# One attention and FFN block in float32r: how the mean and scale of two row blocks are turned and stored, and how attention's pieces are dealt to the FFN pairs

## The chip, the cores and the metric

The kernel runs on one core of a Trainium2 chip. The metric is the device time of one execution in microseconds (us). TensorE does the matrix products, VectorE and ScalarE the work by elements, GpSimd a few small operations and part of the DMA issues, SyncE ("SP") most of the DMA issues. In the profile they are PE (with PEld for its weight loads), DVE, ACT, POOL and SP.

## The reference

The block takes x of 2048 rows and 576 columns, normalizes each row, and adds to x an attention and a feed-forward network (FFN) that both read the normalized rows:

```
xn = (x - mean(x)) / sqrt(var(x) + 1e-5)                # per row, 576 columns
q, k, v = split(xn @ wqkv)                              # 32 heads of 18 columns
logits[s, w] = q[s] . k[s - 2 w] * 18**-0.5             # w = 0..7, earlier rows only
A = (softmax over w of logits, times v[s - 2 w]) @ wo
B = relu(xn @ w1 + b1)**2 @ w2 + b2                     # 4608 hidden columns
out = x + A + B
```

All inputs and the output are float32.

## The kernel before

**Blocks and phases.** The 2048 rows are four blocks of 512 (`TB`). The 4608 hidden columns are 36 tiles of 128, taken as 18 pairs (`NP`). The program runs in this order: `open_rows` and `q0` (normalization and QKV of blocks 0 and 1), `phase_a(0)` (18 FFN pairs for blocks 0 and 1 together, with the output products of block 0), `phase_b0` (output products of block 1, then QKV of blocks 2 and 3 in "quads"), `phase_a(1)` (18 FFN pairs for blocks 2 and 3), `phase_b1` and `tail`.

**Products.** Each float32 operand is split into a high and a low float32r part; ScalarE makes the high part and VectorE the low part by subtraction (`w2_hi` and `w2_lo`, `w1_hi` and `w1_lo`, `square_hi` and `square_lo`). A pair's first products for the two blocks are done with seven products instead of eight (slots T1, T2, T3, T4, B11, B21, B22). The 64 columns of xn that are left over after 512 go into a stacked product of their own; its weights are made by `left_w(r)` for four pairs at a time.

**A pair, `ffn_pair(s, p, work)`.** TensorE goes through `product(ba, B11)`, `product(bc, T1)`, `product(bb, T2)`, `product(bb, T3)`, `product(ba, B21)`, then `third()` with `product(bc, B22)` and `fourth()` with `product(bb, T4)`. Between them `work(i)` adds seven output products at a time (line 549). ScalarE's copy of the first product (line 723) comes once in each pair. VectorE combines the next pair's weights (`combine_w1`), makes the low halves (`splits`), and adds `r1[:, 1] = bc + u` after T3; only then can TensorE go on to write the bank `bc` in `third()` (line 653, which waits for `r`).

**Work beside the pairs.** Each engine works through its own queue in program order. Three kinds of work are laid between a pair's steps:
- Attention. One (block, group) pair of eight heads is a generator of 19 steps, each one VectorE instruction of about 128x1152 elements or a few smaller ones (`attention`, lines 380 to 422). `side(k)` runs k steps. In `phase_a(0)` a pair runs `PIECES[p]` steps in its first part, before `splits`, then two in `third()` and two at its end. In the quads a step is run after the numbers listed at line 1241. `complete(b)` runs what is still left of a block. GpSimd issues attention's loads (lines 362 and 364) and its eight stores of `o` (line 420).
- Mean and scale of blocks 2 and 3, `statistics(b)` (lines 169 to 189). `ROWS` (line 45) places its four steps, one row group of 128 rows each: for block 2 in pairs 7, 8 and 9, for block 3 in pairs 11, 12 and 13; the last step lies in `part(0)` of pair 9 or 13. A step is two `bn_stats`, one `bn_aggr`, a copy of the mean, and `inverse_std`: VectorE adds epsilon (line 153), GpSimd raises to the power -0.5 (line 154). After the last step GpSimd issues the store of the whole `mr` (line 184) to `mrscr[b]` in DRAM, which is laid out [8, 128], while `mr` is [128, 8]: the access pattern is turned, so each contiguous piece is one value of 4 bytes. `load_mb(b)` (line 212) reads `mrscr[b]` back, spread to all partitions, before block b is normalized in `phase_b0`.
- The leftover weights. In part 1 of pairs 1, 5, 9 and 13 SyncE issues the load of `in_w1l` (line 602); in part 0 of pairs 2, 6, 10 and 14 VectorE combines them (`left_w`, four instructions), ScalarE makes the high half in part 1, VectorE the low half in part 2, and GpSimd stores both (line 611).

Parts 0, 1 and 2 are the calls `part(i)` within `ffn_pair`; `part(0)` stands before the `PIECES[p]` steps.

Of the kernel before, what the change touches and what calls it, by code (L numbers as in the profile page):

```python
# [8 lines left out]
F32 = mybir.dt.float32  # L9
# [7 lines left out]
P = 128  # L17
# [4 lines left out]
NJ = TB // P  # L22
# [10 lines left out]
L = P // G  # L33
# [9 lines left out]
NS = 7  # L43
PLAIN = 3
ROWS = {(4 * b - 1 + k // 3, k % 3): (b, h) for b in (2, 3) for k, h in ((0, 0), (2, 2), (3, 1), (5, 2), (6, 2))}
PIECES = (0, 0, 1, 2, 2, 3, 1, 3, 2, 2, 1, 2, 1, 0, 2, 2, 4, 4)
STACK = {T1: 0, B11: 1, B22: 2, B21: 3, T3: 4, T2: 5, T4: 6}


# [1 line left out]
def block_kernel(ctx: ExitStack, tc: tile.TileContext, x, xt, wqkv, wo, w1, b1, w2, b2, w1l, out):  # L51
    nc = tc.nc
    const = ctx.enter_context(tc.tile_pool(name="const", bufs=1))
    mt = ctx.enter_context(tc.tile_pool(name="mt", bufs=1))
    sb = ctx.enter_context(tc.tile_pool(name="sb", bufs=1))
# [24 lines left out]
    half = const.tile([P, 1], F32, name="half")  # L80
# [19 lines left out]
    mrscr = {b: dram.tile([2 * NJ, P], F32, name=f"mr{b}") for b in range(2, NB)}  # L100
# [41 lines left out]
    def bn_stats(b, rows, j, k):  # L142
        if k == 0:
            ln[b, j] = sb.tile([P, 2, 6], F32, name="st6", bufs=NJ)
        nc.vector.bn_stats(out=ln[b, j][:, k], in_=rows[:, j, k * 288:(k + 1) * 288])

    def mean_var(b, j):
        mv = sb.tile([P, 2], F32, name="mv", bufs=NJ)
        nc.vector.bn_aggr(out=mv, in_=ln[b, j])
        ln[b, j] = mv  # L150

    def inverse_std(rs, var):
        nc.vector.tensor_scalar(out=rs, in0=var, scalar1=EPS, scalar2=None, op0=ALU.add)
        nc.gpsimd.tensor_tensor(out=rs, in0=rs, in1=half, op=ALU.pow)
# [14 lines left out]
    def statistics(b):  # L169
        mr = sb.tile([P, 2, NJ], F32, name="mr")  # L170
        for j in range(NJ):
            for k in range(2):
                if b == 1:
                    bn_stats(b, rows_of[b], j, k)
                else:
                    if k == 0:
                        ln[b, j] = sb.tile([P, 2, 6], F32, name="st6", bufs=NJ)
                    nc.vector.bn_stats(out=ln[b, j][:, k], in_=rows_of[b][j][:, 0, k * 288:(k + 1) * 288])
            mean_var(b, j)
            nc.vector.tensor_copy(mr[:, 0, j:j + 1], ln[b, j][:, 0:1])  # L180
            inverse_std(mr[:, 1, j:j + 1], ln[b, j][:, 1:2])
            if j == NJ - 1:
                if b > 1:
                    nc.gpsimd.dma_start(mrscr[b].rearrange("n p -> p n"), mr.rearrange("p k j -> p (k j)"))
                mrs[b] = mr
                measured.add(b)
                if b == 1:
                    release()
            yield
# [177 lines left out]
    def release():  # L367
        free[0] += 1
        fetch()

    def offer(b, g=None):
        if g is None:
            loads.append(("x", b, None))
            queue.append((("x", b), lambda: statistics(b)))
        else:
            loads.extend([("k", b, g), ("v", b, g)])
            queue.append((("k", b, g), lambda: attention(b, g)))
        fetch()
# [47 lines left out]
    def side(k, exp=True):  # L426

        while k > 0:
            if current[0] is None:
                if not queue or queue[0][0] not in landed:  # L430
                    return k
                name, make = queue.pop(0)
                current[:] = [make(), None, name]
            if current[1] == "exp" and not exp:
                return k
            try:
                current[1] = next(current[0])
                k -= 1
            except StopIteration:
                current[0] = None  # L440
        return 0
# [188 lines left out]
    def ffn_pair(s, p, work, first=False):  # L630
# [30 lines left out]
        def part(i):  # L661

            if not s and (p, i) in ROWS:
                b, h = ROWS[p, i]
                if h:
                    next(rv["m", b])
                else:
                    rv["m", b] = statistics(b)
                if h < 2:
                    load_two_rows(b, h)  # L670
# [59 lines left out]
        if not first:  # L730
            side(2 + (p > 2) if s else PIECES[p], False)
        work(0)
# [392 lines left out]
    def phase_b0():  # L1125
        b = 1
# [110 lines left out]
        def quads(k, half, some):  # L1237
            for n in some:
                s, i = steps[n]
                quad_step(k, s, 2 * half + i, i)  # L1240
                if n in ((1, 2, 3, 4, 6, 8, 10, 11, 12), (0, 2, 6, 8, 10, 12, 13), (2, 3, 5, 6, 7, 8, 9, 10, 11, 12, 13), (0,))[2 * k + half]:
                    side(1)
                hook(k, half, s, i)

        for k, half in ((0, 0), (0, 1), (1, 0)):
            quads(k, half, range(len(steps)))
        quads(1, 1, range(len(steps) - 2))

        def chunks(*cs):
# [5 lines left out]
        def filler(i):  # L1255
            if i == 0:
                quads(1, 1, [len(steps) - 2])
# [455 lines left out]
    nc.sync.dma_start(b2t, b2)  # L1713
    load_xt(1)
    of_rows = statistics(1)
    open_rows()
    for g in range(G):
# [66 lines left out]
```

## Time and profile before

| | us |
|---|---|
| median of 3 runs | 1126.09 (1122.3 to 1127.82) |
| profiled execution | 1128.06 |
| its span, first to last instruction | 1126.2 |
| TensorE busy | 1099.2 |
| VectorE busy | 888.3 |
| ScalarE busy | 566.9 |
| GpSimd busy | 153.2 |

Mean granted TensorE clock: 0.988. DMA moved 297.32 MB, 264 GB/s in the mean.

In the tables of the trace a row of the timeline gives the start in us from the span's start, the duration in us, the engine, the line of the kernel, the operation, the tiles written and read, and in brackets the idle time of the engine ahead of the instruction and what ended it. A row of the waits gives who waited for whom: us in total, how many times, the longest. A row of DMA issues gives the tiles, the queue, the count, the size of one and the median time from issue to landing. A row of a stretch gives its limits, its length, the busy us of each engine with the number of instructions in brackets, the granted clock, the mean busy share of the 16 DMA engines, and GB/s. A group by line gives busy us in total, mean ns of one, and idle us ahead of it. Busy time of TensorE is modelled, since matmuls are pipelined.

### The profile page before, as it was taken

What the parts mean: (1) busy time and instruction counts of PE and PEld (TensorE: products, weight loads), DVE (VectorE), ACT (ScalarE), POOL (GpSimd) and SP (SyncE); (2) the same over time, 40 slices, a digit from 0 to 9 for tenths busy, and PEclk for the clock granted to TensorE, in tenths of its full rate; (3) what the DMA queues carried; (4) which work ended last, traced back from release to release, by engine and by line L of the source; (5) the groups of instructions that cost most, each with busy time, mean ns of one, the idle gap of its engine ahead of it and who ended that gap; (6) DMA issues with size and microseconds to landing.
All of it is one profiled execution on the core that took longest, in us unless ns stands there. A gap on an engine that the chain in (4) does not pass through costs nothing.

```text
span 1126.2 us, 13956 instructions
## 1 busy us (share of the span) xinstructions
PE 1099.2 (98%) x4919; PEld 926.4 (82%) x4919; DVE 888.3 (79%) x1195; ACT 566.9 (50%) x801; POOL 153.2 (14%) x278
## 2 busy tenths in 40 slices
PE   9998999999699899999989999999999999999998
PEld 7997888888587788888889988888888888888887
DVE  7966898996796888899979667867768576889955
ACT  5545665665465555465435354545555455544342
POOL 5011220212021020002202110102011010101010
PEclk9999999999899899999999999999999999999999
DMA  8759897897798878877774889687686868685672
GB/s 286 245 191 340 250 371 299 307 368 183 274 336 226 311 268 301 293 235 255 274 232 141 264 329 339 230 298 271 232 308 213 312 218 311 213 280 187 201 277 88
DMA packets 106213, 297.32 MB, mean 264 GB/s; under 512 B 12576, under 2 KB 39456, under 8 KB 95264
## 3 DMA queue, kind: packets, MB, share of 16 engines
q1 hardware_dynamic: 68960, 188.26, 49.4%
q0 software_dynamic: 14080, 67.24, 16.7%
q10 hardware_dynamic: 23104, 40.94, 10.8%
q8 instruction: 38, 0.62, 0.2%
q14 instruction: 31, 0.25, 0.1%
HBM read 211.90 MB, written 84.49 MB: 263 GB/s over the span
## 4 chain that ended last, share of the span: by engine, by line
PE 79%; DVE 8%; DMA 6%; issue 5%; ACT 1%; POOL 0%; SPq 0%; DVEq 0%; POOLq 0%; ACTq 0%
PE p L549 39%; PE p L653 30%; PE p L1081 6%; DMA st<-in_w1l 3%; DVE pr L118 1%; PE p L1085 1%; DVE w1r L118 1%; PE p L1450 1%; DVE w2s L118 1%; DVE w1s L118 1%; DMA st<-xl 1%; PE p L659 1%; DMA xf<-in_xt 1%; DVE r L118 1%; PE p L1540 1%
## 5 line engine op out<-in xcount | busy, mean ns | idle before, releaser
L549 PE MATMUL p<-h,w2s 128*128 128x512 f32 x2066 | 493.5, 391 | 0.0
L549 PEld LDWEIGHTS p<-h,w2s 128*128 128x128 f32 x2066 | 388.8, 188 | 81.9 <-DVE S L957 0.5
L653 PE MATMUL p<-X,w1s 128*128 128x512 f32 x864 | 224.2, 396 | 14.9 <-DVE r L118 14.9
L653 PEld LDWEIGHTS p<-X,w1s 128*128 128x128 f32 x864 | 165.4, 192 | 50.3 <-DVE r L118 15.8
L522 ACT ACTIVATE w2s<-w2r 128x640 fp32r<-128x640 f32 x164 | 120.3, 735 | 135.0 <-PE p L549 97.2
L118 DVE TENSOR_TENSOR w2s<-w2r,w2s 128x576 fp32r<-128x576 f32 (+1 forms) x165 | 124.0, 752 | 75.2 <-ACT w2s L522 75.1
L653 PE MATMUL p<-S,w1s 128*128 128x512 f32 x648 | 166.2, 392 | 2.8 <-DVE r L118 2.8
L653 PEld LDWEIGHTS p<-S,w1s 128*128 128x128 f32 x648 | 122.7, 190 | 28.8 <-DVE r L118 3.2
L420 POOL DMA_DIRECT2D o<-q x128 | 69.4, 608 | 401.4 <-DVE q L118 392.9
L696 ACT ACTIVATE r<-r,b1t 128x512 f32<-128x512 f32 x72 | 52.1, 724 | 136.4 <-DVE r L118 134.6
L118 DVE TENSOR_TENSOR pr<-lg,kv 128x1152 f32<-128x1152 f32 x64 | 86.7, 1354 | 1.2
L118 DVE TENSOR_TENSOR pr<-q,kv 128x1152 f32<-128x1152 f32 x64 | 86.7, 1354 | 1.1
L391 DVE TENSOR_REDUCE lg<-pr 128x64 f32<-128x1152 f32 x64 | 86.4, 1350 | 1.1
L118 DVE TENSOR_TENSOR r<-p,r 128x512 f32<-128x512 f32 (+1 forms) x77 | 53.1, 689 | 36.7 <-PE p L653 16.7
L118 DVE TENSOR_TENSOR pr<-pr 128x576 f32<-128x576 f32 (+1 forms) x128 | 77.6, 606 | 3.3
L704 ACT ACTIVATE r<-r 128x1024 f32<-128x1024 f32 x72 | 76.1, 1057 | 1.2
L738 ACT ACTIVATE r<-p 128x512 f32<-128x512 f32 x36 | 21.5, 598 | 83.3 <-PE p L653 83.3
L118 DVE TENSOR_TENSOR h<-r,h 128x1024 fp32r<-128x1024 f32 (+2 forms) x43 | 49.8, 1163 | 10.9 <-ACT r L704 8.6
L118 DVE TENSOR_TENSOR w1s<-w1r,w1s 128x1024 fp32r<-128x1024 f32 (+2 forms) x42 | 46.2, 1102 | 10.6 <-ACT w1s L491 10.2
L696 ACT ACTIVATE r<-p,b1t 128x512 f32<-128x512 f32 x72 | 48.2, 671 | 0.3 <-PE p L659 0.2
L118 DVE TENSOR_TENSOR h<-h 128x1024 fp32r<-128x1024 f32 x36 | 43.9, 1220 | 1.8 <-ACT h L977 1.7
L549 PE MATMUL p<-w1s,w2s 128*128 128x512 f32 x195 | 44.7, 389 | 0.0
(226 smaller groups left out, 1183.7 us busy)
## 6 DMA issues: line engine op xcount, KB each, us to landing
w2r<-in_w SPq DMA_DIRECT2D x144, 320.0 KB, 3.7
kv<-kvq POOLq DMA_DIRECT2D x32, 1296.0 KB, 8.8
w<-w1s SPq DMA_DIRECT2D x21, 1024.0 KB, 7.9
w1s<-w ACTq DMA_DIRECT2D x19, 1024.0 KB, 6.4
h<-r SPq DMA_DIRECT2D x36, 512.0 KB, 6.2
h<-h SPq DMA_DIRECT2D x36, 512.0 KB, 4.2
w<-w1s SPq DMA_DIRECT2D x15, 768.0 KB, 11.4
w1s<-w ACTq DMA_DIRECT2D x15, 768.0 KB, 5.7
```

Of the source, the lines that this page charges most:

```text
L118: return nc.vector.tensor_tensor(out=out, in0=a, in1=b, op=op)
L391: nc.vector.tensor_reduce(out=lg[:, j * HG:(j + 1) * HG].rearrange("p a w -> p w a"), in_=pr.rearrange("p w (a d) -> p w a d", d=DH), axis ...
L420: nc.gpsimd.dma_start(rows[:, i], q[i * L:(i + 1) * L, :, a:z])
L522: nc.scalar.activation(w2s[stream[i]][:, :DE], raw2[i], AF.Copy)
L549: nc.tensor.matmul(yp[b][c], v, a, start=c not in yb[b], stop=c in last and c not in [o[0] for o in ops[i + 1:]], skip_group_check=True)
L653: nc.tensor.matmul(to, l, r, start=start and i == 0, stop=i == len(mm) - 1, skip_group_check=True)
L659: nc.tensor.matmul(to, weight(LEFT, k, f), v, start=False, stop=k == 1, skip_group_check=True)
L696: nc.scalar.activation(to, a, AF.Relu, bias=b1t[:, f:f + 1])
L704: nc.scalar.activation(r, r, AF.Square)
L738: nc.scalar.activation(u[:, 0], bb, AF.Copy)
L1081: nc.tensor.matmul(to, l[:, js], r, start=start and n == 0, stop=n == len(mm) - 1, skip_group_check=True)
L1085: nc.tensor.matmul(to, v[:, js], ws[LEFT, f][:, n], start=False, stop=n == 1, skip_group_check=True)
```

## The change

The store of `mr` is replaced. VectorE turns `mr` in square blocks of 32 by 32 into a new tile `mrt` of [128, 32]: within each group of 32 partitions, row c then holds value c of the 32 partitions. The eight values are repeated four times to fill the 32 columns. GpSimd then issues four stores, one for each group of 32 partitions, each with 8 rows of 32 values, so pieces of 128 bytes. What lands in `mrscr` is the same as before. The second part changes only where attention's steps run: `PIECES`, and the numbers at line 1241.

```
-PIECES = (0, 0, 1, 2, 2, 3, 1, 3, 2, 2, 1, 2, 1, 0, 2, 2, 4, 4)
+PIECES = (0, 0, 0, 2, 3, 4, 0, 3, 2, 0, 2, 2, 1, 0, 2, 2, 4, 5)
...
                 if b > 1:
-                    nc.gpsimd.dma_start(mrscr[b].rearrange("n p -> p n"), mr.rearrange("p k j -> p (k j)"))
+                    t = sb.tile([P, L], F32, name="mrt")
+                    nc.vector.transpose(t.rearrange("p (n m) -> p n m", m=2 * NJ),
+                                        mr.rearrange("p k j -> p (k j)")[:, None].to_broadcast([P, P // L, 2 * NJ]))
+                    for i in range(P // L):
+                        nc.gpsimd.dma_start(mrscr[b][:, i * L:(i + 1) * L], t[i * L:i * L + 2 * NJ])
...
-                if n in ((1, 2, 3, 4, 6, 8, 10, 11, 12), (0, 2, 6, 8, 10, 12, 13), (2, 3, 5, 6, 7, 8, 9, 10, 11, 12, 13), (0,))[2 * k + half]:
+                if n in ((1, 2, 3, 4, 5, 6, 8, 9, 10, 11, 12), (0, 2, 6, 8, 10, 12, 13), (2, 3, 5, 6, 7, 8, 9, 10, 11, 12, 13), (0, 3))[2 * k + half]:
                     side(1)
```

## The prediction

> **What bounds the kernel now.** I read the page first (span, busy times, chain), then the waits.
>
> ```profile
> span 1126.2 us, 13956 instructions
> ...
> PE 1099.2 (98%) x4919; PEld 926.4 (82%) x4919; DVE 888.3 (79%) x1195; ACT 566.9 (50%) x801; POOL 153.2 (14%) x278
> ```
>
> TensorE (PE) sets the time. A change elsewhere pays only where TensorE stands or runs at a lower clock; it stands for 1126.2 - 1099.2 = 27.0 us in all. Who it stands for is in the view of waits:
>
> ```profile
> DVE st L118 <- DMA st<-in_w1l: 22.4, 3, 12.0
> ...
> PE p L653 <- DVE r L118: 17.8, 3, 9.4
> ...
> POOL o L420 <- DMA mr<-mr: 7.1, 1, 7.1
> ```
>
> TensorE's large wait, 17.8 us in three places, is for VectorE's (DVE's) `r`; VectorE's large wait for a transfer is for `in_w1l`, the leftover weight rows of `left_w`. The store that is changed, mr to mr, is named once, by GpSimd (POOL), which costs nothing. To see whether it has to do with the other two I laid the timeline out around each of the two stores. Block 2 (pairs 9 and 10):
>
> ```profile
> 257.52 0.14 DVE L153 TENSOR_SCALAR mr<-mv 128x1 f32<-128x1 f32 x1
> ...
> 257.74 0.99 POOL L154 TENSOR_TENSOR mr<-mr,half 128x1 f32<-128x1 f32 x1 [5.77 <-DVE mr L153]
> ...
> 259.03 0.95 POOL L184 DMA_DIRECT2D mr<-mr  x1 [0.29 <-POOL mr L154]
> ...
> 267.22 0.56 SPq L602 DMA_DIRECT2D st<-in_w1l  x1
> ...
> 285.52 1.27 DVE L118 TENSOR_TENSOR st<-st 128x128 f32<-128x128 f32 x4 [12.04 <-DMA st<-in_w1l]
> ...
> 290.44 0.69 DVE L118 TENSOR_TENSOR r<-p,r 128x512 f32<-128x512 f32 x1
> ...
> 291.18 2.93 PE L653 MATMUL p<-X,w1s 128*128 128x512 f32 x6 [9.38 <-DVE r L118]
> ```
>
> Block 3 (pairs 13 and 14):
>
> ```profile
> 339.44 0.99 POOL L154 TENSOR_TENSOR mr<-mr,half 128x1 f32<-128x1 f32 x1 [1.77 <-DVE mr L153]
> ...
> 341.65 1.22 DVE L118 TENSOR_TENSOR w1s<-w1r,w1s 128x1024 fp32r<-128x1024 f32 x1 [1.63 <-ACT w1s L491]
> ...
> 346.67 5.31 SPq L602 DMA_DIRECT2D st<-in_w1l  x1
> ...
> 362.43 1.27 DVE L118 TENSOR_TENSOR st<-st 128x128 f32<-128x128 f32 x4 [7.83 <-DMA st<-in_w1l]
> ...
> 369.48 2.93 PE L653 MATMUL p<-X,w1s 128*128 128x512 f32 x6 [5.55 <-DVE r L118]
> ```
>
> Twice the same order: the store, six to eight us later the load of `in_w1l`, VectorE standing in its in-order queue until that load lands, TensorE standing until VectorE has caught up to `r`. The load is issued four times in this phase, in pairs 1, 5, 9 and 13, and only the last two follow a store of `mr`. Landing times by stretch (pairs 1, 5, 9, 13 in order), then two queues over the whole run:
>
> ```profile
> st<-in_w1l SPq DMA_DIRECT2D x1, 256.0 KB, 5.6
> ...
> st<-in_w1l SPq DMA_DIRECT2D x1, 256.0 KB, 7.2
> ...
> st<-in_w1l SPq DMA_DIRECT2D x1, 256.0 KB, 18.2
> ...
> st<-in_w1l SPq DMA_DIRECT2D x1, 256.0 KB, 15.6
> ...
> o<-q POOLq DMA_DIRECT2D x64, 24.0 KB, 3.6
> ...
> mr<-mr POOLq DMA_DIRECT2D x2, 4.0 KB, 12.5
> ```
>
> Busy times by stretch (PE, PEld, DVE, ACT, POOL, then granted clock, DMA share, GB/s):
>
> ```profile
> 260.00:270.00 10.00, 10.00 (x45) 8.29 (x45) 9.93 (x11) 5.09 (x8) 3.80 (x7) 1.00 0.76 32
> ...
> 290.00:295.00 5.00, 3.82 (x9) 3.06 (x10) 4.96 (x6) 2.14 (x3) 1.09 (x2) 0.50 0.96 305
> ...
> 345.00:350.00 5.00, 5.00 (x24) 4.14 (x23) 4.96 (x5) 2.01 (x4) 0.00 (x0) 1.00 1.35 61
> ...
> 400.00:410.00 10.00, 10.00 (x46) 8.13 (x45) 9.90 (x10) 4.92 (x7) 5.45 (x10) 1.00 0.60 164
> ...
> 580.00:590.00 10.00, 10.00 (x53) 9.62 (x52) 7.80 (x11) 4.09 (x8) 0.00 (x0) 1.00 0.84 227
> ```
>
> Behind each store the 16 DMA engines are three quarters busy or more and move 32 and 61 GB/s; the page's mean is 264. So 1024 pieces of 4 bytes (128 partitions by 8 values) fill the engines for some ten us, and everything else that is in flight lands late.
>
> **What the change is worth, part by part.** *The flood goes.* ScalarE's copy of the first product (L723) marks each pair and in a TensorE-bound pair waits for TensorE:
>
> ```profile
> 253.24 0.58 ACT L723 ACTIVATE p<-p 128x512 f32<-128x512 f32 x1
> ...
> 300.35 0.58 ACT L723 ACTIVATE p<-p 128x512 f32<-128x512 f32 x1 [1.26 <-PE p L653]
> ...
> 335.36 0.58 ACT L723 ACTIVATE p<-p 128x512 f32<-128x512 f32 x1 [0.23 <-PE p L653]
> 352.87 0.58 ACT L723 ACTIVATE p<-p 128x512 f32<-128x512 f32 x1 [0.48 <-PE p L653]
> ...
> 378.74 0.58 ACT L723 ACTIVATE p<-p 128x512 f32<-128x512 f32 x1 [1.66 <-PE p L653]
> ```
>
> An undisturbed pair takes 352.87 - 335.36 = 17.51 us. Pairs 9 and 10 take 300.35 - 253.24 = 47.11, which is 12.09 over two pairs. Pair 14 takes 378.74 - 352.87 = 25.87, 8.36 over. Together 20.45 us: the two stands, 9.38 + 5.55 = 14.93, and 5.5 us for matmuls at a granted clock of about half after each (0.50 in the row 290 to 295).
>
> The Trainium skill, page "TensorE: Matmul & The Clock Gate", section "What's actually happening", says that the clock halves after an idle window of about 3.4 us and comes back after about as long a busy one. As an estimate by that page each stand adds 1.7 us, 3.4 for both, and the sum would be 18.3; the pair rows show 2.7 each, and I go by the rows.
>
> Do the stands vanish whole? In block 2 the load, issued at 267.22, would land at 272.8 to 274.4 with the landing times of pairs 1 and 5. VectorE came to it at 285.52 - 12.04 = 273.48. From its start on `st` to the end of `r` it took 290.44 + 0.69 - 285.52 = 5.6 us with one attention piece between; the new deal puts two there, 1.4 more, so 7.0. `r` ends at 280.5 to 281.5, and TensorE began to stand at 291.18 - 9.38 = 281.8: a margin of 0.3 to 1.3 us. In block 3 the load would land by 346.67 + 7.2 = 353.9, before VectorE is there (362.43 - 7.83 = 354.6); 7.05 us from there to TensorE's start gives 361.65 against 369.48 - 5.55 = 363.9. Both vanish, the first by a thin margin.
>
> *The turn, and a new wait.* Costs of a small VectorE instruction and of a transposition, and the attention pieces, from the groups by line; and the store's reader, from the tile's view:
>
> ```profile
> L180 DVE COPY mr<-mv 128x1 f32<-128x1 f32 x12 | 1.8, 154 | 0.5
> ...
> L913 DVE STREAM_TRANSPOSE r<-h 128x512 f32<-128x512 f32 x2 | 1.4, 704 | 0.0
> ...
> L118 DVE TENSOR_TENSOR pr<-q,kv 128x1152 f32<-128x1152 f32 x64 | 86.7, 1354 | 1.1
> ```
>
> ```profile
> L212 SPq DMA_DIRECT2D mb<-mr x1: 326/326/326, 428.1 to 428.1; - x1
> ```
>
> A transposition of 128x32 lies between 0.15 us (a copy of one column) and 0.70 (16 times the columns); I take 0.2, near the copy, for it has 32 columns. But it reads what GpSimd's power writes, so VectorE, which went on at once, now waits: 0.1 to the power's start, 0.99 for it, 0.1 to 0.3 back, in all 1.2 to 1.4. Behind it in VectorE's queue lie the low halves of w2 and w1, for which TensorE waits in the end. In block 3 VectorE stood 1.63 us for ScalarE two instructions later (row 341.65), which hides all of it. In block 2 the new deal takes two pieces, 2.8 us, out of just this place, which is more than the 1.4 that come in. Counted at nothing; without these covers it is 1.6 us each. If GpSimd is behind, the wait grows: in block 3 an attention's stores of `o` stand before the powers, yet GpSimd stood 1.77 us for VectorE there, and in block 2 5.77.
>
> *Four stores for one.* At 0.95 us for an issue, the dearest bound, GpSimd spends 3.8 instead of 0.95 per block. Behind them in its queue lie attention's stores and loads; the 7.1 us that a store of `o` stood goes. Who reads `mr` does so at 428.1, 87 us later. Nothing. Each store has 8 pieces of 128 bytes. The nearest row is that of the small `o` stores, 128 pieces of 192 bytes each, which land in 3.6 us. By pieces the flood shrinks to 32/1024 of ten us, 0.3 us.
>
> The Trainium skill, page "DMA: Bandwidth & Descriptors", section "Specifications", speaks against such pieces: under 512 bytes a transfer is read, modified and written. The trace agrees for 4 bytes (32 GB/s) and does not for 192 (3.6 us).
>
> *The deal.* The sums of PIECES are 32 and 32. Pairs 4, 5, 10 and 17 get one piece more, pairs 2 and 6 one less, pair 9 two less; up to pair 9 it is 14 instead of 16, caught up in the last pair. The tightest is pair 5 with four before its splits; pair 16 has four now, and the row 400 to 410 shows VectorE at 9.90 and TensorE at 10.00 there, so this costs nothing, or at worst 1.4 us in each of pairs 5 and 10. In the QKV quads three pieces come earlier, two of them in a stretch where VectorE is idle 2.2 us in ten (580 to 590): nothing, since TensorE does not stand there.
>
> Sum: 1128.06 for the profiled execution less 20.45 is 1107.6. That execution lies 2.0 above the median 1126.09, so the median becomes 1105.7. For the thin margin of pair 10 I add 0.8: **1106.5**. Bounds of this case: 1105.7 to 1108.5 (1.4 in each of two pairs), and 2.8 for the spread of the median (1122.3 to 1127.82 in three runs), so 1103 to 1111.
>
> **Rivals.** *The load is only half relieved.* For: VectorE is at 9.93 of ten before the stand, and the store is not the only traffic. Against: pairs 1 and 5 have the same traffic without it. With landings halfway, 12.7 and 11.4 us, `r` in block 2 ends at 267.22 + 12.7 + 7.0 = 286.9, a stand of 5.1 with 2.7 for the clock; in block 3 at 346.67 + 11.4 + 7.05 = 365.1, 1.2 late. 9.0 of the gain is lost: 1114.7.
>
> *The change doesn't touch the cause.* The load would be late from the other megabytes in flight. For: a DMA share of 0.96 in other stretches. Against: 32 GB/s at 0.76 is not what megabytes look like. 1126.
>
> *VectorE behind GpSimd, slower.* The transposition waits in pairs 9 and 13 for a power that lies behind GpSimd's blocked queue. A wait of W costs TensorE W less some 2 of margin and 2.7 for the clock, twice; it outweighs 20.4 from W = 9.5 on. For: GpSimd has stood 7.1 us for this ring. Against: it was idle before both powers. With W = 12: 2 x 12.7 - 20.4, 1131.
>
> **How the numbers follow.** Forecast 0.78, half relieved 0.14, cause missed 0.05, behind GpSimd 0.03. A measurement of this kernel tells about 0.5%, 5.6 us, from no change. The first two are faster by more: 0.92; same 0.05; slower 0.03. Range: from 1103 through the forecast's 1111 into the half relief, to 1116.
>
> **What would show it.** Right: `in_w1l` lands in under 9 us in all four pairs, VectorE's wait for it falls from 22.4 to under 6, L723's copies stand 17.5 apart from pair 9 to 15, the clock is 1.00 from 280 to 300, no stretch there is busy at under 100 GB/s. Wrong: a stand of TensorE for `r` in pairs 5, 10 or 11, a VectorE wait over 2 us before the transposition, or late loads without the 4-byte pieces.

## The result, and the profile after

Measured side by side, the changed kernel takes 1104.89 us (median of 6 runs, 1102.51 to 1107.99) and the kernel before 1125.49 (6 runs, 1122.3 to 1127.82): a ratio of 0.9825, 95% interval 0.9801 to 0.985. The profiled execution took 1103.96 us. The first lines of its page:

```profile
span 1102.2 us, 13963 instructions
...
PE 1091.2 (99%) x4919; PEld 920.0 (83%) x4919; DVE 889.3 (81%) x1197; ACT 567.0 (51%) x801; POOL 154.5 (14%) x284
```

TensorE now stands for 1102.2 - 1091.2 = 11.0 us instead of 27.0, and its busy time is 8.0 us shorter for the same 4919 matmuls, because fewer of them run at the half clock (the mean granted clock rises from 0.988 to 0.998). VectorE and GpSimd do slightly more than before. In the code after the change, lines from 185 on have moved by four: L553, L606, L657 and L727 are the old L549, L602, L653 and L723. From the view of waits, and from that of line 606 (the load of `in_w1l`):

```profile
DVE st L118 <- DMA st<-in_w1l: 3.0, 1, 3.0
...
PE p L657 <- DVE r L118: 2.1, 1, 2.1
```

```profile
DMA to landing us min/median/max: 2.7/6.4/7.7
```

TensorE's 17.8 us for `r` are 2.1, VectorE's 22.4 for the load are 3.0, and no landing takes over 7.7 us, where two had taken 18.2 and 15.6. ScalarE's copies of L727, one in each pair; these are pairs 9, 11, 14 and 15:

```profile
250.54 0.58 ACT L727 ACTIVATE p<-p 128x512 f32<-128x512 f32 x1
...
285.55 0.58 ACT L727 ACTIVATE p<-p 128x512 f32<-128x512 f32 x1
...
338.07 0.58 ACT L727 ACTIVATE p<-p 128x512 f32<-128x512 f32 x1 [0.48 <-PE p L657]
355.58 0.58 ACT L727 ACTIVATE p<-p 128x512 f32<-128x512 f32 x1 [0.61 <-PE p L657]
```

Pairs 9 and 10 take 35.01 us together and pair 14 takes 17.51: nothing is left of the 12.09 and 8.36 above an undisturbed pair. The two profiled spans differ by 24.0 us, more than these 20.45; the executions were already 253.24 - 250.54 = 2.70 apart when pair 9 began, ahead of both stores, and the medians differ by 20.6. The stretches of ten us, in the columns of before:

```profile
260.00:270.00 10.00, 10.00 (x46) 8.29 (x45) 9.47 (x13) 6.50 (x9) 4.89 (x9) 1.00 0.95 327
...
290.00:300.00 10.00, 10.00 (x45) 8.23 (x45) 8.71 (x13) 5.58 (x8) 0.56 (x1) 1.00 0.71 240
```

The DMA engines move 327 GB/s where they had moved 32, and the clock is 1.00 where it had been 0.50 (290 to 295 of before). The timeline around the new stores of block 2:

```profile
255.05 0.55 POOL L154 TENSOR_TENSOR mr<-mr,half 128x1 f32<-128x1 f32 x1 [5.77 <-DVE mr L153]
...
255.63 0.21 DVE L185 STREAM_TRANSPOSE mrt<-mr 128x32 f32<-128x32 f32 x1 [0.66 <-POOL mr L154]
...
256.14 2.06 POOL L188 DMA_DIRECT2D mr<-mrt  x4 [0.54 <-DVE mrt L185]
...
262.17 0.33 SPq L606 DMA_DIRECT2D st<-in_w1l  x1
...
262.59 4.35 POOL L424 DMA_DIRECT2D o<-q  x8 [4.39 <-DVE q L118]
...
269.45 0.57 POOL L368 DMA_DIRECT2D kv<-kvq  x1 [2.52 <-DMA o<-q]
...
276.60 0.69 DVE L118 TENSOR_TENSOR r<-p,r 128x512 f32<-128x512 f32 x1 [0.28 <-ACT r L766]
```

Two things matter here. The turn costs VectorE 0.66 us of waiting and 0.21 of work, and the four issues take 2.06 us. And GpSimd's queue: behind its stores lie attention's eight stores of `o`, for which it waits 4.39 us for VectorE, and then the load of v, 1296 KB, at 269.45. These go out behind the load of `in_w1l` (262.17), the last of them after that has landed. The same part of GpSimd's queue before the change:

```profile
259.97 3.82 POOL L420 DMA_DIRECT2D o<-q  x7
...
270.88 0.53 POOL L420 DMA_DIRECT2D o<-q  x1 [7.09 <-DMA mr<-mr]
...
272.16 0.56 POOL L364 DMA_DIRECT2D kv<-kvq  x1 [0.74 <-DMA o<-q]
```

There the 4-byte store held up the eighth store of `o` for 7.09 us and with it the load of v, to 272.16. The experiments turn on these times.

### The profile page after: what moved, and what is told of

Read it like the earlier page. It is cut to its first block, busy times and chain, and to the rows that moved or that the text cites. A ratio compares the mean times of both kernels' runs of the same rounds, so it can differ in the third digit from the quotient of the medians.

```text
span 1102.2 us, 13963 instructions
## 1 busy us (share of the span) xinstructions
PE 1091.2 (99%) x4919; PEld 920.0 (83%) x4919; DVE 889.3 (81%) x1197; ACT 567.0 (51%) x801; POOL 154.5 (14%) x284
## 3 DMA queue, kind: packets, MB, share of 16 engines
q0 software_dynamic: 14272, 67.24, 17.1%
## 4 chain that ended last, share of the span: by engine, by line
PE 91%; issue 3%; DMA 2%; DVE 2%; POOL 0%; ACT 0%; SPq 0%; POOLq 0%; DVEq 0%
PE p L553 44%; PE p L657 34%; PE p L1085 6%; PE p L1544 2%; PE p L1089 1%; PE p L1454 1%; PE p L1599 1%; DMA st<-xl 1%; PE p L663 1%; DVE pr L118 1%; DMA xf<-in_xt 1%; DMA kvq<-st 0%; PE p L1371 0%; POOL kvq L1099 0%; DVE w2s L118 0%
## 5 line engine op out<-in xcount | busy, mean ns | idle before, releaser
L553 PE MATMUL p<-h,w2s 128*128 128x512 f32 x2066 | 491.8, 389 | 0.2 <-ACT h L704 0.2
L553 PEld LDWEIGHTS p<-h,w2s 128*128 128x128 f32 x2066 | 387.6, 188 | 81.9 <-ACT h L704 0.6
L657 PE MATMUL p<-X,w1s 128*128 128x512 f32 x864 | 219.3, 389 | 0.0
L657 PEld LDWEIGHTS p<-X,w1s 128*128 128x128 f32 x864 | 162.1, 188 | 33.7
L657 PE MATMUL p<-S,w1s 128*128 128x512 f32 x648 | 164.8, 390 | 2.1 <-DVE r L118 2.1
L657 PEld LDWEIGHTS p<-S,w1s 128*128 128x128 f32 x648 | 121.5, 188 | 28.1 <-DVE r L118 2.5
L118 DVE TENSOR_TENSOR r<-p,r 128x512 f32<-128x512 f32 (+1 forms) x77 | 53.1, 690 | 37.1 <-ACT r L766 17.1
L553 PE MATMUL p<-w1s,w2s 128*128 128x512 f32 x195 | 44.7, 389 | 0.0
```

The lines of the kernel that those rows point to most:

```text
L118: return nc.vector.tensor_tensor(out=out, in0=a, in1=b, op=op)
L553: nc.tensor.matmul(yp[b][c], v, a, start=c not in yb[b], stop=c in last and c not in [o[0] for o in ops[i + 1:]], skip_group_check=True)
L657: nc.tensor.matmul(to, l, r, start=start and i == 0, stop=i == len(mm) - 1, skip_group_check=True)
```

## The experiments

My theory was that of the prediction: the 4-byte pieces fill the DMA engines, and their going is the whole gain. The rivals: the deal has a part in it, or the turned layout matters and not the pieces. The kernel before ran beside each of three sets of runs, at 1121.99, 1123.4 and 1122.41 us; ratios are to the one of the same set.

**The store alone** (the old deal stays)

```
-                    nc.gpsimd.dma_start(mrscr[b].rearrange("n p -> p n"), mr...)
+                    t = sb.tile([P, L], F32, name="mrt")
+                    nc.vector.transpose(...)
+                    for i in range(P // L):
+                        nc.gpsimd.dma_start(mrscr[b][:, i * L:(i + 1) * L], t[i * L:i * L + 2 * NJ])
```

> The turn and the four stores, with the old deal of attention's pieces. Flood theory (the 4-byte pieces hold up every transfer, so in_w1l lands late): in_w1l lands in under 9 us in pairs 9 and 13, VectorE's wait for it falls from 22.4 us to under 6, and 18 to 21 us of the 20.6 are gained, 1104 to 1108; what is missing is the new wait of VectorE (0.7 to 1.4 us twice) where two pieces still stand in pair 9. Deal theory (two pieces fewer in pair 9 give VectorE the lead that TensorE needs): hardly any gain, 1120 to 1127.

Measured: 1110.68 us, ratio 0.9897 (0.9868 to 0.9926). That is 11.3 us of gain, not 20. The timeline:

```profile
251.82 0.58 ACT L727 ACTIVATE p<-p 128x512 f32<-128x512 f32 x1
...
259.46 4.37 POOL L424 DMA_DIRECT2D o<-q  x8
...
263.60 0.79 POOL L368 DMA_DIRECT2D kv<-kvq  x1
...
266.79 0.33 SPq L606 DMA_DIRECT2D st<-in_w1l  x1
...
278.92 1.27 DVE L118 TENSOR_TENSOR st<-st 128x128 f32<-128x128 f32 x4 [6.00 <-DMA st<-in_w1l]
...
284.57 2.93 PE L657 MATMUL p<-X,w1s 128*128 128x512 f32 x6 [3.63 <-DVE r L118]
...
294.09 0.58 ACT L727 ACTIVATE p<-p 128x512 f32<-128x512 f32 x1 [1.61 <-PE p L657]
```

Block 3 is clean: the load of pair 13 lands in 7.7 us. In pair 9 it still takes 12.0 without a single 4-byte piece, VectorE stands 6.00 us, TensorE 3.63, and the half clock follows again (0.50 from 284 to 288); pairs 9 and 10 take 294.09 - 251.82 = 42.27, which is 7.25 above two undisturbed ones. So something else makes it late in block 2. GpSimd's rows offer a cause: nothing holds it up any more, and the load of v goes out at 263.60, 3.2 us ahead of `in_w1l`, where it had gone out 4.9 us behind (272.16 and 267.22). A second one is that `in_w1l` itself is issued late, 14.97 us behind ScalarE's copy of that pair, against 11.63 with the whole change.

**The deal alone** (the old store stays; `PIECES` and the quads as in the change)

```
-PIECES = (0, 0, 1, 2, 2, 3, 1, 3, 2, 2, 1, 2, 1, 0, 2, 2, 4, 4)
+PIECES = (0, 0, 0, 2, 3, 4, 0, 3, 2, 0, 2, 2, 1, 0, 2, 2, 4, 5)
```

> The new deal with the old store of 4-byte pieces. Flood theory: in_w1l still lands after 15 to 18 us, TensorE still stands near 9 and 5 us, 1123 to 1130 (one piece more between in_w1l and r in pair 10 may add 1.4). Deal theory: most of the gain, 1105 to 1112.

Measured: 1120.08 us, ratio 0.9983 (0.9968 to 0.9999). Landings, and TensorE's stand in block 2:

```profile
DMA to landing us min/median/max: 3.7/7.9/14.0
```

```profile
286.11 2.93 PE L653 MATMUL p<-X,w1s 128*128 128x512 f32 x6 [7.15 <-DVE r L118]
```

The 14.0 is pair 9 (18.2 before), pair 13 is at 10.5 (15.6 before). Both stands are smaller and both remain: the deal alone brings almost nothing by the median, and the two parts together bring more than their sum (11.3 + 1.9 against 20.6).

**The pieces alone: 32 bytes instead of 4, nothing turned** (old deal; `mr` is stored as it lies, 128 rows of 8 values, so blocks 2 and 3 read their means and scales back in the wrong order)

```
-                    nc.gpsimd.dma_start(mrscr[b].rearrange("n p -> p n"), mr...)
+                    nc.gpsimd.dma_start(dims(mrscr[b], 0, [2 * NJ, P], [1, 2 * NJ]), mr...)
```

> The kernel before with one edit: mr is stored as it lies, 128 pieces of 32 bytes in one store, no turn, so the means and scales of blocks 2 and 3 are used in the wrong order. Flood by pieces: an eighth of the pieces, so an eighth of the flood (about 1.3 us), in_w1l within 9 us, 1104 to 1108. If any store at this place holds up GpSimd's ring or the queues: no gain, 1120 to 1127. If the turn itself or the new wait is what helps: no gain either.

Measured: 1109.18 us, ratio 0.9883 (0.9864 to 0.9903), as with the store alone. The store in block 2, and the load of `in_w1l`:

```profile
mr<-mr POOLq DMA_DIRECT2D x1, 4.0 KB, 1.7
```

```profile
DMA to landing us min/median/max: 3.8/7.4/11.9
```

The same 4 KB, from the same tile, by the same engine, land in 1.7 us as 128 pieces, where 1024 pieces took 11.6 in this place (in block 3: 6.0 against 13.4). Turning has no effect of its own that the time shows. The pieces are fewer and larger at once here, as in the change, so no run says whether their number or their size counts. Again block 3 is clean, and pair 9's load takes 11.9.

**The 4-byte store twice** (the second goes to a scratch that nobody reads)

```
                     nc.gpsimd.dma_start(mrscr[b].rearrange("n p -> p n"), mr...)
+                    nc.gpsimd.dma_start(mrtwo[b].rearrange("n p -> p n"), mr...)
```

> The kernel before with the 4-byte store issued twice, the second time into a scratch that nobody reads. Flood theory: twice the pieces, so in_w1l lands some 10 us later still in pairs 9 and 13 (26 to 30 us), and TensorE stands some 8 to 12 us longer at each: 1140 to 1152. If the lateness has another cause: 1124 to 1131.

Measured, in a single execution: 1133.73 us against 1121.99, so 11.7 slower, between what was expected by the two theories. The two blocks differ:

```profile
265.90 0.45 SPq L604 DMA_DIRECT2D st<-in_w1l  x1
...
268.29 0.53 POOL L422 DMA_DIRECT2D o<-q  x1 [5.60 <-DMA mr<-mr]
...
270.32 0.56 POOL L366 DMA_DIRECT2D kv<-kvq  x1 [0.54 <-DMA o<-q]
...
284.07 1.27 DVE L119 TENSOR_TENSOR st<-st 128x128 f32<-128x128 f32 x4 [12.05 <-DMA st<-in_w1l]
...
368.90 1.27 DVE L119 TENSOR_TENSOR st<-st 128x128 f32<-128x128 f32 x4 [16.33 <-DMA st<-in_w1l]
```

In block 3 the stand doubles, 16.33 us against 7.83. In block 2 it stays at 12.05 (12.04 before), with the load of v behind that of `in_w1l` as before. Block 3 speaks for the flood; block 2 speaks neither for nor against it, and the last section comes back to it.

**Only pair 9 dealt anew** (the store alone, and its two steps moved from pair 9 to pairs 10 and 17)

```
-PIECES = (0, 0, 1, 2, 2, 3, 1, 3, 2, 2, 1, 2, 1, 0, 2, 2, 4, 4)
+PIECES = (0, 0, 1, 2, 2, 3, 1, 3, 2, 0, 2, 2, 1, 0, 2, 2, 4, 5)
```

> The turn and the four stores with the old deal, except that pair 9's two steps go to pairs 10 and 17; the other pairs and the quads as before. If the deal is worth what it is by pair 9 alone: as the whole change, ratio to before 0.98 to 0.985, in_w1l in pair 9 in under 8 us. If the other moves (pairs 2, 4, 5, 6, quads) matter: it stays between 0.985 and 0.99.

Measured: 1106.38 us, ratio 0.9857 (0.9836 to 0.9877), and the longest landing of `in_w1l` is 7.3 us. Pairs 9 and 10 take 35.01 us again (ScalarE's copies at 251.05 and 286.06). Two steps taken out of this one place are the deal's whole part in the gain, within what the runs can tell. They delay the load of v (to 269.35) and hasten the issue of `in_w1l` (262.69, 11.64 us behind the copy), both; the next two runs are there to part these.

**The same traffic, behind the load in program order** (the store alone; the eight stores of `o` of that group, and the v load after them, moved in the program to behind the issue of `in_w1l`)

```
-                ... eight dma_start of o; release()
+                def issue(): ... the same
+                if (b, g) == (0, 2): moved.append(issue)
+                else: issue()
...
+            if moved and p > 8:
+                moved.pop()()
```

> The turn and the four stores with the old deal, and one edit: the eight stores of o and the load of the next v (1296 KB) that follow attention's last step in pair 9 are issued by GpSimd in the pair's third part, behind SyncE's issue of in_w1l; VectorE's steps stay where they are. If the old deal costs by that traffic ahead of in_w1l: it lands in 6 to 8 us instead of 12.0, TensorE's stand in pair 10 falls from 3.6 us to under 1, 1103 to 1107. If it costs by VectorE's two more steps (a later issue of in_w1l, less lead): the stand stays, 1108 to 1113.

Measured: 1110.73 us, ratio 0.9894 (0.9876 to 0.9912). Inconclusive: GpSimd had nothing before these issues in its queue to wait for, so they went out at 258.24 as ever, and the load of v at 262.38, ahead of `in_w1l` at 265.62, which landed in 11.9 us. A place in the program is not a place in time.

**The same traffic, really held** (as above, and GpSimd first copies one column of VectorE's newest attention product, so that it waits for VectorE's step behind the load)

```
+                nc.gpsimd.tensor_copy(sb.tile([P, 32], F32, name="nm", bufs=2)[:, :1], latest[0][:, 0, :1])
                 moved.pop()()
```

> The turn and the four stores with the old deal, as in the run of the stores alone (1110.68), but GpSimd first copies one column of the newest attention product, so that the eight stores of o of block 0's third group and the next load of v go out only after VectorE's step in the last part of pair 9, behind the issue of in_w1l. If the load was late in pair 9 because this traffic went out ahead of it, it now lands in 6 to 8 us after its issue, VectorE doesn't stand in pair 10, pairs 9 and 10 take 35.0 to 36 us, and the time is 1103 to 1107. If it was late because it was issued 3.3 us later, behind a busier VectorE, the landing stays at 10 us or more or the stand in pair 10 stays above 2 us, and the time is 1108 to 1113.

Measured: 1105.4 us, ratio 0.985 (0.9831 to 0.9869). The timeline, with ScalarE's copies of pairs 9 and 11:

```profile
250.59 0.58 ACT L734 ACTIVATE p<-p 128x512 f32<-128x512 f32 x1
...
264.49 0.33 SPq L613 DMA_DIRECT2D st<-in_w1l  x1
...
265.55 4.35 POOL L427 DMA_DIRECT2D o<-q  x8
...
272.49 0.57 POOL L369 DMA_DIRECT2D kv<-kvq  x1 [2.59 <-DMA o<-q]
272.52 1.27 DVE L118 TENSOR_TENSOR st<-st 128x128 f32<-128x128 f32 x4 [0.84 <-DMA st<-in_w1l]
...
286.15 0.58 ACT L734 ACTIVATE p<-p 128x512 f32<-128x512 f32 x1
```

With the old deal, `in_w1l` issued 13.90 us behind ScalarE's copy (14.97 with the store alone), the load lands in 7.9 us, VectorE stands 0.84, and the two pairs take 35.56. That it went out a little earlier in its pair is not the reason: with the pieces of 32 bytes it was issued 14.13 us behind the copy (264.57 and 250.44), with the load of v 3.4 us ahead of it, and took 11.9. What the load had to share the engines with shows in the bytes moved from its issue to its landing, first with the store alone, then with the traffic held:

```profile
266.80:278.80 12.00, 12.00 (x55) 9.88 (x54) 5.69 (x7) 8.86 (x12) 0.55 (x1) 1.00 0.99 369
```

```profile
264.50:272.40 7.90, 7.90 (x36) 6.54 (x35) 6.75 (x8) 5.59 (x7) 4.48 (x9) 1.00 0.98 353
```

The engines are full in both. 12.0 us by 369 GB/s is 4.43 MB, 7.9 by 353 is 2.79: 1.64 MB less. GpSimd's queue in the same two stretches (packets, MB, share of the 16 engines' time):

```profile
q0 software_dynamic: 293, 1.67, 39.5%
...
q0 software_dynamic: 240, 0.28, 10.0%
```

So 1.39 of the 1.64 MB are on GpSimd's queue. The load of v alone is 1296 KB, 1.33 MB; most of the 288 KB of stores of `o` had moved before `in_w1l` was issued with the store alone (0.25 MB on that queue from 259.4 to 266.8), and the rest of the 1.67 fits the load of q, 288 KB, which was issued behind `in_w1l` (270.62) and still moved in its stretch. The load was late because this traffic, by the bytes above all the load of v, moved while it was on its way. Stores and load were held together; which of them would have been enough was not tried.

**The load a part earlier, the 4-byte store kept** (old deal, old store; `in_w1l` issued in part 0 of pairs 9 and 13)

```
-            if i == 1 and p % G == 1 and G * r < NP:
+            if i == (0 if p > 8 else 1) and p % G == 1 and G * r < NP:
```

> The kernel before, old store and old deal, with one edit: in pairs 9 and 13 the load of in_w1l is issued in the pair's first part, right after the last statistics, so about when the 4-byte store is issued or a little ahead. If the flood costs only by making this one load late, it lands before the flood or early enough, and nearly all is gained with the 4-byte pieces still there: 1103 to 1109. If the flood holds up other loads just as much (w2, w1, the stacked weights): in_w1l is in time but TensorE still stands, 1112 to 1124.

Measured: 1104.78 us, ratio 0.9842 (0.982 to 0.9863).

```profile
254.65 0.33 SPq L602 DMA_DIRECT2D st<-in_w1l  x1
...
256.49 0.95 POOL L184 DMA_DIRECT2D mr<-mr  x1 [0.29 <-POOL mr L154]
```

```profile
mr<-mr POOLq DMA_DIRECT2D x1, 4.0 KB, 10.8
```

The store in 4-byte pieces is there and lands in 10.8 us (16.3 in block 3; 11.6 and 13.4 before), and nearly the whole gain is there too: the load went out 1.8 us ahead of it and landed in 3.0. So, within what the runs can tell, the store cost TensorE time by this one load alone.

**The load a part earlier, with the store alone, and with the whole change** (the same edit on each)

> The turn and the four stores with the old deal, and in_w1l issued in the first part of pairs 9 and 13. If the deal works only through the landing of in_w1l: as the whole change, ratio to before 0.98 to 0.985, VectorE's wait for in_w1l near nothing in pairs 10 and 14. If the deal works through VectorE's load in pairs 9 and 10: no better than with the store alone, 0.988 to 0.991.

> The whole change, and in_w1l issued one part earlier in pairs 9 and 13. If all that is lost there is that load's lateness, nothing is left to gain: within 0.2% of the whole change, 1102 to 1107, the load landing in 3 to 6 us. If the whole change still loses time to a thin margin in pair 10: 1 to 2 us better than the whole change.

Measured: 1104.47 us, ratio 0.9836 (0.9819 to 0.9853), and 1104.47, ratio 0.985 (0.9826 to 0.9873). Neither can be told from the whole change (0.9801 to 0.985). Once this load is in time, neither the pieces nor the deal has anything left to bring that these runs can measure.

**The 4-byte store in another place** (the kernel before; the store moved to part 2 of pairs 10 and 14, behind the use of `in_w1l`)

```
+                    late[b] = mr
...
+            if not s and i == 2 and p % 4 == 2 and p // 4 in late:
+                b = p // 4
+                nc.gpsimd.dma_start(mrscr[b].rearrange("n p -> p n"), late[b]...)
```

> The kernel before, old deal, with its store in 4-byte pieces moved from pairs 9 and 13 to the last part of pairs 10 and 14, behind the load of in_w1l and the combination of its weights. If that load alone is sensitive: in block 3 no stand, in block 2 the stand of the stores alone with the old deal (load at about 12 us), so 1108 to 1113. If the pieces delay whatever is in flight enough to matter: new stands of TensorE of 3 us or more behind pairs 10 and 14, for weights of w1 or w2, and 1115 to 1126.

Measured: 1111.26 us, ratio 0.9902 (0.9876 to 0.9929): the time of the store alone. Block 2's remaining stand (the load lands in 11.3 us there), and the loads of w2 and w1 issued behind the second store (352.6):

```profile
277.73 1.27 DVE L118 TENSOR_TENSOR st<-st 128x128 f32<-128x128 f32 x4 [5.19 <-DMA st<-in_w1l]
```

```profile
w2r<-in_w SPq DMA_DIRECT2D x2, 320.0 KB, 14.2
w1r<-in_w SPq DMA_DIRECT2D x1, 512.0 KB, 16.9
```

The flood delays what is issued there about as much as it did before (14.4 and 17.8 us in block 2), and TensorE doesn't notice in block 3; in block 2 there is one stand of 1.15 us, two pairs later, whose cause was not looked for. The weights of w1 and w2 have slack enough for this, `in_w1l` has not.

**The quads as before** (the whole change, but the old numbers in the quads)

```
-                if n in ((1, 2, 3, 4, 5, 6, 8, 9, 10, 11, 12), ..., (0, 3))[2 * k + half]:
+                if n in ((1, 2, 3, 4, 6, 8, 10, 11, 12), ..., (0,))[2 * k + half]:
```

> The whole change, but with the old numbers in the quads, so that three steps of attention run later there. All theories that look for the gain in pairs 9, 10 and 14: nothing, 1103 to 1107, the ratio to the kernel before 0.980 to 0.985. If the quads have a part in the gain: slower than the whole change by 2 us or more.

Measured: 1103.78 us, ratio 0.9838 (0.9817 to 0.9859). The quads' part of the deal does nothing that can be measured.

## Why the prediction was right or wrong

The time came out 1.6 us under the forecast, inside its range. The chain behind a late load was right: VectorE stands, TensorE stands, and the half clock follows. What failed is what the change does to GpSimd's transfers, and two errors there cancelled; in this the total is luck. The prediction named late loads without the 4-byte pieces as a sign of being wrong, and the store alone shows one (12.0 us). There is luck in the size too: the 20.45 us were read from an execution of 1128.06, slower than all 33 other executions of the kernel before (1119.25 to 1127.82), and beside 1122.41 the change without its quads gained 18.6.

- **What bounds the kernel: right.** Both stands vanish whole, 12.09 and 8.36 us by the pair rows, and with them TensorE's half clock. As an estimate by the Trainium skill's "TensorE: Matmul & The Clock Gate", "What's actually happening", a stand was to cost 1.7 us on top of itself. The pair rows of before gave 2.7; the deal alone shows 9.28 us over in block 2 for a stand of 7.15, so 2.1, and the store alone 7.25 for stands of 3.63 and 0.24, so 3.4. The medians can't tell the sum by that estimate, 18.3, from the one by the rows, 20.45: the interval of the ratio is 16.9 to 22.4 us of gain and holds both.
- **"The flood goes": right for the flood, not enough for the load.** That the store in 4-byte pieces holds up the others for some ten us was right; the pieces of 32 bytes and the doubled store in block 3 show it (block 2 took the second store at no cost). That the load would then land within the times of pairs 1 and 5 was wrong in block 2: with the store alone it takes 12.0 us. I wrote that these pairs "have the same traffic without it". They have not. In pair 1 the stores of `o` go out 20.1 us behind `in_w1l` (148.93 and 128.84), in pair 5 they go out 5.2 us behind it, as these rows of the kernel before show:

```profile
194.98 0.60 SPq L602 DMA_DIRECT2D st<-in_w1l  x1
...
200.15 1.64 POOL L420 DMA_DIRECT2D o<-q  x3 [30.62 <-DVE q L118]
```

- **"Four stores for one ... the 7.1 us that a store of `o` stood goes ... Nothing": the step that failed.** The issues do cost nothing (2.06 us, where I had 3.8 at the dearest). But that stall was what kept the load of v behind `in_w1l`. When it goes, and nothing else changes, v goes out 7.1 us earlier in its pair (18.92 us behind ScalarE's copy at 253.24 before, 11.78 behind that at 251.82 with the store alone), ahead of `in_w1l`, and a stand of 3.63 us takes the place of the 9.38. I followed the stall to its end and not to what was queued behind it.
- **"The deal ... Nothing": wrong too, with the other sign.** It undoes just that. Two steps fewer in pair 9 are worth 0.9897 - 0.9857 = 0.4% of the time, some 4.5 us, and the whole change stands 0.7% below the store alone (by medians; the intervals of the ratios are 0.4 to 0.6% wide). Of the deal's two effects there (`in_w1l` earlier in its pair, attention's transfers later) the held traffic shows that the second is enough. I had looked at the deal as work for VectorE and not as what sets when GpSimd's transfers go out. With both steps counted at nothing, the forecast's total came out the same.
- **The half-relieved rival** described, at 0.14, what the store alone does in block 2 (a landing of 12.0 us, where it had 12.7), for the cause that its "for" named: the store is not the only traffic.
- **The thin margin of pair 10:** no stand there, `r` ends 277.29, and the 0.8 us that I added were not needed. The load went out earlier than I had it, again by the deal.
- **The turn and its wait: right.** 0.21 us against 0.2; the wait is 0.66 and not 1.2 to 1.4, because the power took 0.55 and not 0.99. Neither shows in the pairs.
- **The pieces of 128 bytes: right.** The four stores of block 2 land in a median of 2.6 us. By the Trainium skill's "DMA: Bandwidth & Descriptors", "Specifications", pieces under 512 bytes are read, modified and written; at 128 bytes and 32 pieces no cost of that can be seen here.
- **The quads: right**, nothing.

So the total was right because the change removes one cause, sets free a second, and takes that out of the way too. Not settled: why the two parts together bring more than their sum by the medians. Part of it can be the kernel before, which took 1125.49 beside the whole change and 1121.99 beside the parts: against 1121.99, the change's 1104.89 would be a gain of 17.1 and not 20.6. The landings add up (in pair 9 the new store takes 6.2 us off with the old deal and 7.6 with the new), and by the pair rows the deal alone would be worth 6.9 us, but its median shows 1.9; its profiled execution, 1118.01, lies 2.1 below that median.

## What to carry to other kernels

When a load lands late, list what was issued around it on all queues, in order of time, and the bytes that each queue moved from its issue to its landing: with full DMA engines (353 to 369 GB/s here) 1.6 MB more meant 4.1 us more, and another place "has the same traffic" only if it has it in the same order. When a stall of an issuing engine goes, ask which transfers were queued behind it and what they will now run ahead of; and a change in where compute steps stand also moves the DMAs that wait for them. Before anything is removed, ask which transfer has no slack: issuing that one a part earlier is one line, and was worth as much here as the whole change.

## What the runs showed of the hardware

The 4-byte store doesn't slow the other transfers by a share: while it lasts, next to nothing moves. Two stretches of before, during the store of block 2 and just after it landed (259.0 to some 271):

```profile
264.00:268.00 4.00, 4.00 (x20) 3.30 (x19) 3.96 (x5) 1.17 (x3) 0.00 (x0) 1.00 0.70 35
...
272.00:276.00 4.00, 4.00 (x20) 3.27 (x19) 1.42 (x3) 2.03 (x4) 0.56 (x1) 1.00 1.02 397
```

35 GB/s, then 397. What was issued in those 11.6 us landed behind them. The store itself hardly shows as work: from 255 to 275 GpSimd's queue has 8.7% of the engines' time and SyncE's 56.7%. It is the low rate at a high share, and the late landings of the others, that give it away; how the pieces hold the others up is not shown. The stores of `o` show the same, in the stretch after the store, before and after the change:

```profile
o<-q POOLq DMA_DIRECT2D x4, 48.0 KB, 12.0
```

```profile
o<-q POOLq DMA_DIRECT2D x4, 48.0 KB, 5.5
```

Two such stores issued back to back (257.56 and 258.51) landed in 10.4 and 10.2 us in block 2, where one alone had taken 11.6, and in 18.4 and 21.7 in block 3, where one had taken 13.4. Why block 2 took the second at no cost is open.
